# Attention mixer on one core: attention weights in whole products, and the middle of the program planned anew

## Chip, core and metric

One Trainium2 chip, one core. The metric is device time in microseconds (us). The kernel before takes 738.98 us (median of 3 runs, 738.47 to 741.72).

## What is computed

Memory attention in 8 batches of 8 heads, and then a token and channel mixer over the result, all in float32:

```python
a = softmax(phi, axis=2)                       # (8, 8, 576, 32), over the sequence
k_m = einsum('bhsm,bhsd->bhmd', a, k); v_m = einsum('bhsm,bhsd->bhmd', a, v)
attn = softmax(q @ k_m.T / 8)                  # (8, 8, 576, 32)
x = (attn @ v_m) as (8, 576, 512)
h = relu(x.T @ w_tok1) @ w_tok2; u = x + h.T
out = u + relu(u @ w_ch1) @ w_ch2              # 512 -> 1536 -> 512
```

## The kernel before

Float32 accuracy comes from splitting each operand into a high part (rounded by a copy on ACT) and a low part (source minus high, on DVE or POOL); a product is then three products: high by high, high by low, low by high.

**Quads.** Attention goes by quads of four heads: quad `b_Q` is half `Q` of batch `b`. In the middle of the program stand 12 of them, 2_0 to 7_1 (`ThirdBatchQuad` and `LateQuad`). One quad's steps on PE are: `get_kv` (keys and values, 20 narrow products, L452), `turn_T` (L676), `scores` (8 products of 64 rows by 32 columns, L492), `A` (L566), `R` (L572), and for each half of the sequence `attend` (L752) and two `u` (L761). Between them ACT and DVE do softmax and splits, POOL subtracts maxima from `phi` and makes one low part, and the softmax's result goes out to memory and back (`rows_out` L545, `rows_in` L696) to stand in natural order for `A`.

`attend` multiplies the values by the attention weights. The four heads of a quad lie in two pairs of 64 partitions, so each of its six products contracts over 64 rows only, and those of the two pairs (`db` 0 and 1) go to two halves of the array. `a_high` copies all 128 partitions of `aT` on ACT, `a_low` subtracts on DVE.

**Mixer.** The first and second channel layers of chunks 0 to 2 (L146, L169: products of 128 by 128 by 512) are the filler between the quads' steps. Chunks 3 to 8 follow in three pairs (`Pair`, `Run`) by a Strassen scheme, whose weights come as units of 512 KB from memory (`load_unit`, L416): `AHEAD` = 3 units are issued before a run, and then one at each first use of a unit (`Run.first`).

**Order of the work.** `plan` is a list scheduler that runs when the program is built: each `step` has an engine, a cost in us, what it comes after, the rooms (buffers) that it takes, and a rank; `do(t, ...)` gives a quad's step the rank of `t` us after that quad's start, 15.5 us from quad to quad. Engines then run in that order, each strictly in order. `SLACK` is added to what PE and SP wait for, `margin` to a transfer's landing. SP issues nearly all loads; one buffer holds `kv`, so a quad's `kv` is issued only when the quad before it has done `get_kv`. `phi` and the banks `at` and `ch` (two PSUM banks each) have two buffers.

```python
def attend(s, hf):                                   # L745
    w = slice(hf * HALF, (hf + 1) * HALF)
    for x, (v, a) in enumerate(((s.vh, s.ah), (s.vh, s.al), (s.vl, s.ah))):
        for db in range(2):
            own, m = slice(64 * db, 64 * db + 64), slice(db * P, (db + 1) * P)
            nc.tensor.matmul(s.up[db, hf][:, :HALF], v[own, m], a[own, w], start=x == 0, stop=False)
```

Of the kernel before, what the change touches and what calls it, by code (L numbers as in the profile page):

```python
# [10 lines left out]
F32 = mybir.dt.float32  # L11
# [17 lines left out]
def kernel(  # L29
# [37 lines left out]
    WIN, AHEAD = 3, 3  # L67
# [541 lines left out]
    class LateQuad(Quad):  # L609
# [26 lines left out]
        def max_out(s):  # L636
            s.top = dram.tile([1, 4 * M], F32, name="top" + s.n, tag="maxima", bufs=2)
            nc.sync.dma_start(
                out=s.top.rearrange("a (i m) -> (a i) m", m=M), in_=s.turned[:: P // 4, M : 2 * M]
            )  # L640

        def max_in(s):
            s.r = sb.tile([P, 4 * M], F32, tag="pr", name="prr" + s.n, bufs=2)
            nc.sync.dma_start(out=s.r, in_=s.top.to_broadcast([P, 4 * M]))
# [68 lines left out]
        def a_high(s):  # L713
            s.ah = sb.tile([P, S], F32R, tag="ah", name="ah" + s.n, bufs=2)
            nc.scalar.copy(out=s.ah, in_=s.aT)

        def a_low(s, eng):
            s.al = sb.tile([P, S], F32R, tag="ah", name="al" + s.n, bufs=2)
            eng.tensor_tensor(out=s.al, in0=s.aT, in1=f32(s.ah), op=ALU.subtract)
# [25 lines left out]
        def attend(s, hf):  # L745
            w = slice(hf * HALF, (hf + 1) * HALF)
            for db in range(2):
                s.up[db, hf] = bank([P, 512], f"u{db}{hf}" + s.n)
            for x, (v, a) in enumerate(((s.vh, s.ah), (s.vh, s.al), (s.vl, s.ah))):
                for db in range(2):  # L750
                    own, m = slice(64 * db, 64 * db + 64), slice(db * P, (db + 1) * P)
                    nc.tensor.matmul(s.up[db, hf][:, :HALF], v[own, m], a[own, w], start=x == 0, stop=False)  # L752

        def u(s, db, hf):
            m, w = slice(db * P, (db + 1) * P), slice(hf * HALF, (hf + 1) * HALF)
            mm = []
            for t in range(NT):
                h, l = s.Rh[:, t, m], s.Rl[:, t, m]
                mm += [(h, w2h[:, t, w]), (h, w2l[:, t, w]), (l, w2h[:, t, w])]
            for x, (a, r) in enumerate(mm):  # L760
                nc.tensor.matmul(s.up[db, hf][:, :HALF], a, r, start=False, stop=x == len(mm) - 1)  # L761
# [216 lines left out]
    def plan(rank, ways, slow=None, slack=0.0, margin=0.85):  # L978
# [37 lines left out]
        while left:  # L1016
# [4 lines left out]
            if not first:  # L1021
                for z in left:
                    print("STUCK", z.eng, z.fn and z.fn.__code__.co_firstlineno, getattr(getattr(z.fn,"__self__",None),"n",""), z.fn and z.fn.__defaults__, [(r.tags, [(q.tag, sum(u.end is None for u in q.users)) for q in taken.get(r.tags[0][0], [])][-4:]) for r in z.take])
# [594 lines left out]
    class ThirdBatchQuad(SecondQuad):  # L1618

        for name in (  # L1620
            "turn_T", "get_kb", "scores", "S_take", "turn_S", "rows_in", "nat_low", "a_high", "a_low",
            "A", "R", "attend", "u", "straight", "u_high", "u_low", "spill", "store_u",
        ):
            locals()[name] = vars(LateQuad)[name]
# [163 lines left out]
    for z in order:  # L1788
        if z.eng == "PE":
            if z is products[0]:  # L1790
                break
            begin = max(idle, 2.0)
            if z.begin - begin > 0.3 and z.take:

                cold = max(min(z.begin, 5.1) - idle - 1.6, 0.0)
                pace = 0.222 if z.begin < 12.0 else 0.24
                z.fill = int(cold / 0.43 + 0.9 * (z.begin - max(begin, 5.1)) / pace)
            idle = z.end
    for z in order:
        now[0] = z  # L1800
        if z.fn:
            z.fn()

# [3 lines left out]
    def room(tag, n=1):  # L1807
# [8 lines left out]
    kv2, q2, pt2 = room("kv"), room("qT"), room("aT")  # L1816
    begin = step(
        "END", 0, None,
        take=[*sum(c1_rooms, []), *u_rooms[1], o_rooms[0], rest_room, *hidden[0, NF - 1], kv2, q2, pt2],
# [30 lines left out]
    SLACK = 0.4  # L1850
# [8 lines left out]
    def A_LOW(qd):  # L1859
        return "DVE", 0.82, lambda: qd.a_low(nc.vector)  # L1860

    late = [second] + [LateQuad(2, 1)] + [LateQuad(b, Q) for b in range(3, B) for Q in range(2)]
    second_u, former, ends = [], [], {}
    u_done = []
    PERIOD, START, behind, scored, vlows = 15.5, 3.0, [], [begin], []
    for n, qd in enumerate(late):
        t0 = START + PERIOD * n

        def do(t, *args, **kw):
            return todo_at(t0 + t, *args, **kw)  # L1870

        bk, kb, vh, vl, vb, T = room("ch", 2), room("kb"), room("vh", 2), room("vl", 2), Room(("side vb", 1), ("vb", 1)), room("kb") if n else room("pr", 2)
        per = room("ps", 3)
        if n:
            phi_room, kv_r, q_r = room("phi", 2), room("kv"), room("qT")
            r, turned = room("pr", 2), room("al", 2)
            y = do(-32, "SP", 0.45, qd.load_turned, scored[max(n - 2, 0)], take=[turned], move=0.8)
            y.tail = 8.0 if n > 1 else 4.0
            y = do(-27, "DVE", 0.85, qd.phi_max, y, use=[turned])
            y = do(-26, "SP", 0.45, qd.max_out, y, use=[turned], move=0.01)  # L1880
            y.lands, y.tail = True, 2.4
            z = do(-26, "SP", 0.45, qd.load_phi, begin, take=[phi_room], move=0.9)
            y = do(-22, "SP", 0.45, qd.max_in, y, z, take=[r], move=0.1)
            z = do(-16, *PHI_SUB(qd), y, z, use=[phi_room, r], port=True)
            e = do(-13, "ACT", 0.8, qd.phi_only_exp, z, use=[phi_room])
            l = do(-20, "SP", 0.45, qd.load_kv, begin, take=[kv_r], move=3.5)
            lq = do(-12, "SP", 0.45, qd.load_q, begin, take=[q_r], move=1.6)
            kvuse, after = [phi_room, kv_r], [e, l]
        else:
            kvuse, after, q_r, lq = [pt2, kv2], [begin], q2, begin  # L1890
        z = do(-9, "PE", 0.7, qd.get_kv, *after, *former, take=[bk], use=kvuse)
# [12 lines left out]
        aT, ah, al = room("aT"), room("ah", 2), room("ah", 2)  # L1904
        z = do(0, "PE", 1.05, qd.scores, y, lq, take=[*ss, S_], use=[q_r, kb])
        z.not_before = t0
        former, vlows = [z, *vlows[-1:]], vlows + [vlow]
        scored.append(z)
        ends["kv"] = [z]
# [16 lines left out]
        y = do(13, "ACT", 0.7, qd.a_high, t, take=[ah, al], use=[aT])  # L1926
        turned = [y, do(14, *A_LOW(qd), y, use=[aT, ah, al], port=True)]
# [6 lines left out]
        z = do(18, "PE", 0.8, qd.R, z, vlow, *behind, take=[rp], use=[Ah, Al, vh, vl])  # L1934
        z = do(19, "ACT", 0.61, qd.R_high, z, take=[Rh], use=[rp])
        z = do(20, "DVE", 0.7, qd.R_low, z, take=[Rl], use=[rp, Rh])
        last, wrote, stage = z, [[], []], [room(f"stage{db}") for db in range(2)]
        for hf in range(2):
            bks = [room("at", 2) for db in range(2)]
            last = do(20.5 + 2 * hf, "PE", 0.45, lambda qd=qd, hf=hf: qd.attend(hf), z, last, *turned, take=bks, use=[vh, vl, ah, al])  # L1940
            behind = [last]
            n_, to = qd.straight(hf)
            wants = n_ < HALF
            for db, bk in enumerate(bks):
                last = do(
                    21 + 2 * hf + db, "PE", 0.8, lambda qd=qd, db=db, hf=hf: qd.u(db, hf), last, use=[bk, Rh, Rl]
                )
# [145 lines left out]
    order = plan(key, dict.fromkeys(steps, 0), None, SLACK, 2.5)  # L2093
# [43 lines left out]
    class Run:  # L2137
# [151 lines left out]
        def layer_2(s):  # L2289
# [177 lines left out]
```

## Time and profile before

| | |
|---|---|
| median of 3 runs | 738.98 us |
| the profiled execution | 739.23 us, of which 737.4 us are span |
| granted TensorE clock | 0.999 of full speed |
| PE busy | 718.0 us, 4371 products |
| DVE, ACT, POOL busy | 512.5, 349.8, 93.6 us |
| transfers | 155.25 MB, mean 211 GB/s |

Busy time of PE overlaps from product to product, so what a product costs is read from the distance between starts, and what is lost from the waits. A row of the timeline has the start, the duration, the engine, line, operation, output and inputs, rows by columns of the array, the shape, how many, and in brackets the idle time before it and what ended it. The first 120 us hold the loads and quads 0_0 to 1_1; the 12 quads of the middle run from 123 to 380, the three Strassen runs from 383 to the end.

### The profile page before, as it was taken

To read this page: it belongs to the slowest core of one execution; us is meant where nothing else is said; L and a number is where in the kernel's file an instruction comes from. 1 tells how busy PE (TensorE), PEld (TensorE's weight loads), DVE (VectorE), ACT (ScalarE), POOL (GpSimd) and SP (SyncE) were. 2 spreads that over 40 slices of the span, in tenths; PEclk is the share of its full clock that TensorE was granted. 3 is DMA by queue.
4 is the path that set the end of the run, shared out by engine and by line. 5 is a ranking of instruction groups with operands and counts; after the bars stand their busy time and mean duration, and the time that the engine had idled before them with its cause. 6 is when DMAs were issued, how large, how long until landed. Compare 5 with 4: busy or idle time off the path is not lost.

```text
span 737.4 us, 11507 instructions
## 1 busy us (share of the span) xinstructions
PE 718.0 (97%) x4371; PEld 585.7 (79%) x4371; DVE 512.5 (70%) x841; ACT 349.8 (47%) x627; POOL 93.6 (13%) x82
## 2 busy tenths in 40 slices
PE   8999999999999999899997999999999999999998
PEld 8787788777787777688886788887788888788887
DVE  4999854878878797356885648976237977425983
ACT  5999665234344443243443445434345442436450
POOL 2213344222213521100400000000000000000000
PEclk9999999999999999999999999999999999999999
DMA  9965632787979999962436877065559154668302
GB/s 355 415 243 177 219 109 75 235 301 224 289 221 281 322 324 299 321 170 49 163 126 242 304 214 287 29 257 164 185 178 340 48 202 141 199 195 276 129 29 85
DMA packets 99198, 155.25 MB, mean 211 GB/s; under 512 B 38984, under 2 KB 65608, under 8 KB 94792
## 3 DMA queue, kind: packets, MB, share of 16 engines
q1 hardware_dynamic: 88632, 121.37, 48.5%
q10 hardware_dynamic: 10512, 33.17, 14.3%
q8 instruction: 34, 0.56, 0.3%
q14 instruction: 20, 0.16, 0.1%
HBM read 117.34 MB, written 37.16 MB: 210 GB/s over the span
## 4 chain that ended last, share of the span: by engine, by line
PE 63%; DMA 9%; DVE 8%; issue 1%; ACT 1%; POOL 1%; SPq 0%; DVEq 0%; POOLq 0%
PE ma L292 10%; PE mU L2251 10%; PE mB L2251 7%; PE acc L169 6%; PE cp L146 6%; DMA unit<-sums 5%; PE mc L292 5%; PE u L761 4%; PE mD L2251 3%; PE mA L2251 3%; PE Ap L566 2%; PE mb L292 2%; PE u L752 1%; DMA phi<-in_phi_dram 1%; PE kvp L452 1%
## 5 line engine op out<-in xcount | busy, mean ns | idle before, releaser
L169 PE MATMUL acc<-hh,c 128*128 128x512 f32 x288 | 100.0, 396 | 0.0
L169 PEld LDWEIGHTS acc<-hh,c 128*128 128x128 f32 x288 | 54.1, 188 | 12.7 <-issue 2.0
L169 PE MATMUL acc<-hl,c 128*128 128x512 f32 x144 | 56.3, 391 | 0.0
L146 PE MATMUL cp<-uh,c1h 128*128 128x512 f32 x144 | 52.9, 408 | 0.0
L146 PE MATMUL cp<-ul,c1h 128*128 128x512 f32 x144 | 50.5, 391 | 0.0
L146 PE MATMUL cp<-uh,c1l 128*128 128x512 f32 x144 | 50.4, 391 | 0.0
L2237 ACT CAST rT<-hid 128x512 fp32r<-128x512 f32 x54 | 32.0, 621 | 26.8 <-PE mB L2251 15.6
L2238 DVE TENSOR_TENSOR rT<-hid,rT 128x512 fp32r<-128x512 f32 x54 | 35.9, 690 | 7.0 <-ACT rT L2237 7.0
L2105 DVE TENSOR_TENSOR hid<-mb,hid 128x512 f32<-128x512 f32 x12 | 8.3, 692 | 44.6 <-ACT hid L2185 44.6
L711 POOL TENSOR_TENSOR nat<-side,nat 128x512 fp32r<-128x512 f32 (+1 forms) x24 | 24.6, 1026 | 105.7 <-ACT nat L703 99.4
L115 ACT ACTIVATE hh<-cp 128x512 fp32r<-128x512 f32 x36 | 21.5, 596 | 34.3 <-PE cp L146 34.2
L118 DVE SCALAR_TENSOR_TENSOR hl<-cp,hh 128x512 fp32r<-128x512 f32 x36 | 24.6, 684 | 14.0 <-ACT hh L115 14.0
L146 PEld LDWEIGHTS cp<-uh,c1h 128*128 128x128 f32 x144 | 26.5, 189 | 9.4 <-issue 4.9
L2108 ACT ACTIVATE hid<-hid 128x512 f32<-128x512 f32 x24 | 15.2, 633 | 36.2 <-DVE hid L2105 36.2
L146 PEld LDWEIGHTS cp<-uh,c1l 128*128 128x128 f32 x144 | 27.0, 188 | 6.0
L761 PE MATMUL u<-w2h,Rh 128*128 128x288 f32 x96 | 30.8, 321 | 0.0
L146 PEld LDWEIGHTS cp<-ul,c1h 128*128 128x128 f32 x144 | 27.1, 188 | 4.6
L169 PEld LDWEIGHTS acc<-hl,c 128*128 128x128 f32 x144 | 27.1, 188 | 4.4
L292 PE MATMUL ma<-xrest_p,unit 128*128 128x512 f32 x108 | 28.0, 394 | 1.6 <-DMA unit<-sums 1.3
L2237 ACT CAST r<-hid 128x512 fp32r<-128x512 f32 x36 | 22.4, 623 | 14.2 <-PE mU L2251 5.4
L292 PE MATMUL mc<-xw2h_p,unit 128*128 128x512 f32 x72 | 24.6, 395 | 4.5 <-DMA unit<-sums 4.5
L647 POOL TENSOR_TENSOR phi<-phi,prr 128x640 f32<-128x640 f32 x11 | 18.7, 1704 | 80.2 <-DMA prr<-top 33.5
(375 smaller groups left out, 1912.9 us busy)
## 6 DMA issues: line engine op xcount, KB each, us to landing
unit<-sums ACTq DMA_DIRECT2D x54, 512.0 KB, 5.3
kv<-in_kv_dram SPq DMA_DIRECT2D x12, 1300.0 KB, 7.1
rawc<-in_w_ch_dram SPq DMA_DIRECT2D x12, 1024.0 KB, 7.1
q<-in_q_dram SPq DMA_DIRECT2D x16, 576.0 KB, 5.2
sums<-sums SPq DMA_DIRECT2D x12, 512.0 KB, 8.7
u_p<-spilled SPq DMA_DIRECT2D x6, 1024.0 KB, 7.1
phi<-in_phi_dram SPq DMA_DIRECT2D x16, 320.0 KB, 7.5
unit<-sums ACTq DMA_DIRECT2D x18, 256.0 KB, 3.5
```

The lines of the kernel that those rows point to most:

```text
L115: nc.scalar.activation(out=h, in_=ps, func=AF.Relu)
L118: nc.vector.scalar_tensor_tensor(out=l, in0=ps, scalar=0.0, in1=f32(h), op0=ALU.max, op1=ALU.subtract)
L146: nc.tensor.matmul(ps, l[:, a, w], r[:, a], start=n == 0, stop=n == len(mm) - 1)
L169: nc.tensor.matmul(ps, l_[f // 2][:, f % 2, a * P : (a + 1) * P], r[:, w], start=f == start and x == 0, stop=f == end - 1 and x == 2,)
L292: nc.tensor.matmul(ps, l, r, start=first and n == 0, stop=n == len(mm) - 1, skip_group_check=not first,)
L647: eng.tensor_tensor(out=s.pt, in0=s.pt, in1=s.r.rearrange("p (i m) -> p i m", i=4) .unsqueeze(2) .to_broadcast([P, 4, NC, M]), op=ALU.subt ...
L711: eng.tensor_tensor(out=o, in0=a, in1=f32(h), op=ALU.subtract)
L761: nc.tensor.matmul(s.up[db, hf][:, :HALF], a, r, start=False, stop=x == len(mm) - 1)
L2108: nc.scalar.activation(out=to, in_=x, func=AF.Relu)
L2237: nc.scalar.copy(out=t[:, 0], in_=x)
L2238: nc.vector.tensor_tensor(out=t[:, 1], in0=x, in1=f32(t[:, 0]), op=ALU.subtract)
L2251: nc.tensor.matmul(s.banks[room][a][:, w], l_[:, a * P : a * P + P], r_, start=not (p or x) and name in ("11", "T1", "21", "T4"), stop=p = ...
```

## The change

- `attend` goes. `a_high` and `a_low` write, for each pair `p`, one tile of 128 partitions with the pair's high parts in its own 64 partitions and the low parts in the other 64; `v_pair` (four copies of 64 by 128 on ACT) lays the high values twice, one above the other. One product of 128 rows then gives high by high plus high by low, a second one low values by the same tile; both stand at the head of `u`, which starts its own group. `v_pair` is planned behind `R_high`.
- `get_kv` of the next quad is planned directly behind `scores` of this one.
- The middle's ranks: `phi`, its maxima and `kv` are ranked 4 to 12 us earlier, the transposed `phi` of quad 2_1 and its maximum are issued before the middle. `SLACK` 0.4 to 0.8, `margin` 2.5 to 3.5, and `BEHIND`: the planner lets SP issue nothing while landings are more than 2.5 us behind. No instruction waits for that; it sets the order.
- `AHEAD` 3 to 4: four units are issued before the first run, and four instead of three (at steps 35 to 38) before each of the others.

```diff
-    WIN, AHEAD = 3, 3
+    WIN, AHEAD = 3, 4
...
+        def a_high(s, p):
+            if not p:
+                s.pairs = [sb.tile([P, S], F32R, tag="ah", name=f"a{x}" + s.n, bufs=2) for x in range(2)]
+            own = slice(64 * p, 64 * p + 64)
+            nc.scalar.copy(out=s.pairs[p][own], in_=s.aT[own])
+
+        def a_low(s, p, eng):
+            own, other = slice(64 * p, 64 * p + 64), slice(64 - 64 * p, P - 64 * p)
+            t = s.pairs[p]
+            eng.tensor_tensor(out=t[other], in0=s.aT[own], in1=f32(t[own]), op=ALU.subtract)
+
+        def v_pair(s, p):
+            if not p:
+                s.vv = sb.tile([P, 2, P], F32R, tag="Al", name="vv" + s.n, bufs=1)
+            own = slice(64 * p, 64 * p + 64)
+            for x in range(2):
+                nc.scalar.copy(out=s.vv[64 * x : 64 * x + 64, p], in_=f32(s.vh[own, p * P : p * P + P]))
...
         def u(s, db, hf):
+            s.up[db, hf] = bank([P, 512], f"u{db}{hf}" + s.n)
             m, w = slice(db * P, (db + 1) * P), slice(hf * HALF, (hf + 1) * HALF)
-            mm = []
+            a = s.pairs[db][:, w]
+            mm = [(s.vv[:, db], a), (s.vl[:, m], a)]
...
+            if z.eng == "SP":
+                t = max(t, landed.get("SP", 0.0) - behind)
...
+        z = do(0, "PE", 1.0, qd.scores, y, qd.lq, take=[*ss, S_], use=[qd.q_r, kb])
+        if nx:
+            got_kv = do(0.1, "PE", 1.25, nx.get_kv, z, *nx.after, *vlows[-1:], take=[bank_rooms[n + 1]], use=nx.kvuse)
...
-                    (35, load_unit), (36, load_unit), (37, load_unit),
+                    (35, load_unit), (36, load_unit), (37, load_unit), (38, load_unit),
```

On PE, where quad 4_1 multiplies its values by the attention weights; before (names are tile, batch, quad, number):

```order
L752 MATMUL u00_4_1_3002<-ah_4_1_2870,vh_4_1_2614 128x288
L752 MATMUL u10_4_1_3003<-ah_4_1_2870,vh_4_1_2614 128x288
L752 MATMUL u00_4_1_3002<-al_4_1_2900,vh_4_1_2614 128x288
L752 MATMUL u10_4_1_3003<-al_4_1_2900,vh_4_1_2614 128x288
L752 MATMUL u00_4_1_3002<-ah_4_1_2870,vl_4_1_2625 128x288
L752 MATMUL u10_4_1_3003<-ah_4_1_2870,vl_4_1_2625 128x288
L761 MATMUL u00_4_1_3002<-w2h_96,Rh_4_1_2957 128x288
```

and of the change:

```order
L764 MATMUL u00_4_1_3103<-a0_4_1_2851,vv_4_1_3076 128x288
L764 MATMUL u00_4_1_3103<-a0_4_1_2851,vl_4_1_2678 128x288
L764 MATMUL u00_4_1_3103<-w2h_96,Rh_4_1_3068 128x288
L764 MATMUL u00_4_1_3103<-w2l_97,Rh_4_1_3068 128x288
L764 MATMUL u00_4_1_3103<-w2h_96,Rl_4_1_3079 128x288
```

Six products of half the rows ahead of two `u` have become two whole ones at the head of each `u`; the four `u` of a quad now mostly stand back to back. From the last product of `R` to the first of `u` there are 6 to 15 mixer products before (most often 9; in four quads `get_kv` besides), and now 15, or 9 to 12 and `get_kv` or an `A` besides.

On PE, the scores of quad 6_0 (`sp`) and the keys and values of 6_1 (`kvp`); before:

```order
L492 MATMUL sp1_6_0_3145<-q_6_0_2951,kb_6_0_3092 32x288
L146 MATMUL cp2_2_3128<-uh_2_1385,c1h2_611 128x512
L146 MATMUL cp2_2_3128<-ul_2_1386,c1h2_611 128x512
L146 MATMUL cp2_2_3128<-uh_2_1385,c1l2_612 128x512
L146 MATMUL cp2_2_3128<-uh_2_1385,c1h2_611 128x512
```

and of the change:

```order
L492 MATMUL sp0_6_0_3199<-q_6_0_2933,kb_6_0_2981 32x288
L492 MATMUL sp1_6_0_3200<-q_6_0_2933,kb_6_0_2981 32x288
L452 MATMUL kvp_6_1_3214<-kv_6_1_2945,phi_6_1_2854 32x130 x20
L572 MATMUL Rp_5_0_3242<-vh_5_0_2781,Ah_5_0_3179 128x256
L572 MATMUL Rp_5_0_3242<-vl_5_0_2849,Ah_5_0_3179 128x256
```

Before, `kvp` of 6_1 stood 13 rows behind these scores, after mixer products and an `R`. Of 11 such places 7 are joined now; before, 3 were, and one `get_kv` stood directly before an `attend`.

On ACT, the unit loads where the first Strassen run begins; before:

```order
L416 DMA unit011_4299<-sums1_1380 128x1024
L2185 COPY hidal_0_4295<-ma00_4315 128x512
L2108 ACTIVATE hidal_0_4295<-hidal_0_4295 128x512
L416 DMA unit002_4335<-sums0_1379 128x1024
L2191 COPY hidal_0_4296<-mc00_4334 128x512
L2194 COPY hidaT_0_4297<-ma00_4315 128x512
L416 DMA unit012_4353<-sums1_1380 128x1024
```

and of the change:

```order
L416 DMA unit002_4337<-sums0_1385 128x1024
L2216 COPY hidal_0_4333<-ma00_4353 128x512
L2139 ACTIVATE hidal_0_4333<-hidal_0_4333 128x512
L416 DMA unit012_4373<-sums1_1386 128x1024
L2222 COPY hidal_0_4334<-mc00_4372 128x512
L2225 COPY hidaT_0_4335<-ma00_4353 128x512
L416 DMA unit020_4391<-sums2_1387 128x1024
```

Each unit's load stands where the one before it stood.

## Rows read from the trace of the kernel before

**Rows 1.** The page: busy time of each engine, share of the span, instructions.

```profile
PE 718.0 (97%) x4371; PEld 585.7 (79%) x4371; DVE 512.5 (70%) x841; ACT 349.8 (47%) x627; POOL 93.6 (13%) x82
```

**Rows 2.** Waits of PE, 60 to 400: who for whom, us, times, longest.

```profile
PE mc L292 <- DMA unit<-sums: 3.9, 2, 2.1
PE kvp L452 <- ACT phi L446: 3.3, 2, 1.8
PE u L752 <- DVE Rl L118: 2.2, 1, 2.2
...
PE kvp L676 <- DVE side L1145: 0.2, 1, 0.2
```

**Rows 3.** Waits of PE, 400 to the end.

```profile
PE ma L292 <- DMA unit<-sums: 1.3, 3, 0.6
PE mc L292 <- DMA unit<-sums: 0.6, 2, 0.4
```

**Rows 4.** Timeline of PE: the keys of 7_1, and a product that waits for a unit.

```profile
314.10 1.32 PE L452 MATMUL kvp<-kv,phi 128*32 128x130 f32 x40 [1.49 <-ACT phi L446]
...
396.54 0.39 PE L292 MATMUL mc<-xw2h_p,unit 128*128 128x512 f32 x1
398.75 0.47 PE L292 MATMUL mc<-xw2h_p,unit 128*128 128x512 f32 x1 [1.82 <-DMA unit<-sums]
```

**Rows 5.** Stretches: length, busy PE, PEld, DVE, ACT, POOL; clock, DMA share, GB/s.

```profile
125.00:225.00 100.00, 99.36 (x768) 77.99 (x768) 77.49 (x145) 36.36 (x79) 19.58 (x15) 1.00 0.83 259
225.00:303.00 78.00, 73.82 (x632) 58.03 (x630) 60.07 (x109) 32.48 (x70) 20.46 (x16) 1.00 0.97 308
```

**Rows 6.** Timeline of PE around one `attend`.

```profile
190.23 0.39 PE L146 MATMUL cp<-ul,c1h 128*128 128x512 f32 x1
190.46 0.39 PE L146 MATMUL cp<-uh,c1l 128*128 128x512 f32 x1
190.78 0.40 PE L752 MATMUL u<-ah,vh 64*128 64x288 f32 x2
...
191.61 0.29 PE L761 MATMUL u<-w2l,Rh 128*128 128x288 f32 x1
191.74 0.29 PE L761 MATMUL u<-w2h,Rl 128*128 128x288 f32 x1
```

**Rows 7.** Timeline of PE: scores alone, keys alone, both joined (last four rows).

```profile
198.78 0.39 PE L169 MATMUL acc<-hh,c 128*128 128x512 f32 x1
...
200.08 0.39 PE L146 MATMUL cp<-ul,c1h 128*128 128x512 f32 x1
...
207.53 0.39 PE L169 MATMUL acc<-hh,c 128*128 128x512 f32 x1
...
209.43 0.39 PE L146 MATMUL cp<-ul,c1h 128*128 128x512 f32 x1
...
172.05 0.39 PE L146 MATMUL cp<-uh,c1l 128*128 128x512 f32 x1
172.37 0.72 PE L492 MATMUL sp<-q,kb 64*32 64x288 f32 x16
173.02 1.32 PE L452 MATMUL kvp<-kv,phi 128*32 128x130 f32 x40
...
174.60 0.39 PE L146 MATMUL cp<-ul,c1h 128*128 128x512 f32 x1
```

**Rows 8.** Groups on ACT, 30 to 130: quads 1_0 and 1_1, already in pairs.

```profile
L1524 ACT CAST a<-aT 64x576 fp32r<-64x576 f32 x4 | 2.7, 674 | 0.2
...
L538 ACT CAST vv<-vh 64x128 fp32r<-64x128 f32 x8 | 2.4, 298 | 0.1
```

**Rows 9.** High and low attention weights, L715 and L719: ns least, median, most.

```profile
L715 ACT CAST ah<-aT x12: 668/671/677, 139.6 to 351.5; 128x576 fp32r<-128x576 f32 x12
...
L719 DVE TENSOR_TENSOR al<-aT,ah x12: 743/758/1662, 140.3 to 352.8; 128x576 fp32r<-128x576 f32 x12
```

**Rows 10.** Timeline of ACT's queue: loads of units as the first run begins.

```profile
383.81 0.33 ACTq L416 DMA_DIRECT2D unit<-sums  x1
...
387.95 0.84 ACTq L416 DMA_DIRECT2D unit<-sums  x2
```

More of the change, by code (lines that the diff above doesn't have):

```diff
@@ L1798 @@
             idle = z.end
+    late = [second] + [LateQuad(2, 1)] + [LateQuad(b, Q) for b in range(3, B) for Q in range(2)]
+    ahead = [(quads[1, 0].x_u[3].end, late[1].load_turned)] + [(118.0, fn) for fn in (late[1].phi_max, late[1].max_out)]
     for z in order:
+        while ahead and z.begin > ahead[0][0]:
+            ahead.pop(0)[1]()
         now[0] = z
@@ L1802 @@
             z.fn()
+    assert not ahead
     steps.clear()
@@ L1816 @@
     kv2, q2, pt2 = room("kv"), room("qT"), room("aT")
+    turned1 = room("al", 2)
     begin = step(
         "END", 0, None,
[L1819 removed]
+        take=[*sum(c1_rooms, []), *u_rooms[1], o_rooms[0], rest_room, *hidden[0, NF - 1], kv2, q2, pt2, turned1],
     )
@@ L1857, in NAT_LOW @@
         return "POOL", 1.8, lambda: qd.nat_low(nc.gpsimd)
[L1859 to L1865, printed above, removed]
-    for n, qd in enumerate(late):
[L1867 to L1880, printed above, removed]
-            y.lands, y.tail = True, 2.4
[L1882 to L1891, printed above, removed]
@@ new lines, with later @@
+    second_u, ends, u_done = [], {}, []
+    PERIOD, START = 15.5, 3.0
+    first, scored, vlows, ahead = [begin], [begin], [], []
+    bank_rooms = [room("ch", 2) for qd in late]
+    kb_rooms, vh_rooms, vl_rooms = ([room(tag, m) for qd in late] for tag, m in (("kb", 1), ("vh", 2), ("vl", 2)))
+    def later(n):
+        t0 = START + PERIOD * n
+        return t0, lambda t, *args, **kw: todo_at(t0 + t, *args, **kw)
+    for n, qd in enumerate(late):
+        t0, do = later(n)
+        if not n:
+            qd.kvuse, qd.after, qd.q_r, qd.lq = [pt2, kv2], [begin], q2, begin
+            continue
+        phi_room, kv_r, q_r = room("phi", 2), room("kv"), room("qT")
+        if n == 1:
+            y, turned = begin, turned1
+        else:
+            turned = room("al", 2)
+            y = qd.l_turned = do(TURN_AT, "SP", 0.45, qd.load_turned, begin, take=[turned], move=0.8)
+            y.tail = 8.0 if n > 2 else 4.0
+            y = do(-36, "DVE", 0.85, qd.phi_max, y, use=[turned])
+            y = do(-35, "SP", 0.45, qd.max_out, y, use=[turned], move=0.01)
+            y.lands, y.tail = True, 2.4
+        z = do(-30, "SP", 0.45, qd.load_phi, begin, take=[phi_room], move=0.9)
+        r = room("pr", 2)
+        y = do(-28, "SP", 0.45, qd.max_in, y, z, take=[r], move=0.1)
+        z = do(-21, *PHI_SUB(qd), y, z, use=[phi_room, r], port=True)
+        e = do(-20, "ACT", 0.8, qd.phi_only_exp, z, use=[phi_room])
+        l = do(-28, "SP", 0.45, qd.load_kv, begin, take=[kv_r], move=3.5)
+        qd.lq = do(-12, "SP", 0.45, qd.load_q, begin, take=[q_r], move=1.6)
+        qd.kvuse, qd.after, qd.q_r = [phi_room, kv_r], [e, l], q_r
@@ L1892 @@
+    t0, do = later(0)
+    got_kv = do(-9, "PE", 1.25, second.get_kv, begin, take=[bank_rooms[0]], use=second.kvuse)
+    for n, qd in enumerate(late):
+        t0, do = later(n)
+        bk, kb, vh, vl, vb = bank_rooms[n], kb_rooms[n], vh_rooms[n], vl_rooms[n], Room(("side vb", 1), ("vb", 1))
+        T, per = room("kb") if n else room("pr", 2), room("ps", 3)
+        z = got_kv
         if n:
@@ L1925 @@
         ends["S"] = [t, z]
-        y = do(13, "ACT", 0.7, qd.a_high, t, take=[ah, al], use=[aT])
-        turned = [y, do(14, *A_LOW(qd), y, use=[aT, ah, al], port=True)]
+        turned = []
+        for p in range(2):
+            y = do(12 + p, "ACT", 0.69, lambda qd=qd, p=p: qd.a_high(p), t, *turned[:1], use=[aT, *ah] if p else [aT], take=[] if p else ah)
+            turned += [y, do(14 + p, "DVE", 0.8, lambda qd=qd, p=p: qd.a_low(p, nc.vector), y, use=[aT, *ah], port=True)]
         ap, Ah, Al = room("at", 2), room("Ah"), room("Al")
```

77 lines of the change are left out of this document (35 added, 42 removed).

## The prediction

> **What bounds the kernel now.** I read the page's first part, then PE's waits, then PE's timeline at the places that the change touches, then the stretches. PE is busy 718.0 of 737.4 us [rows 1]: it is the bound, and a gain is either less PE work or fewer PE waits. PE's waits have two kinds. From 60 to 400 there are eight entries, 11.3 us in all, of which the first three and the last stand here [rows 2]: 3.9 us are two waits for units of the Strassen run, and 7.4 us belong to the quads, chiefly keys that wait for `exp(phi)` (3.3 us) and a `u` that waits for `R`'s low part (2.2 us). Behind 400, five more waits for units cost 1.9 us [rows 3]. The view undercounts: the wait shown as 1.82 us lies between starts 2.21 us apart, where 0.23 is usual, so it costs 1.98, or 0.16 more [rows 4, 6]. With 0.16 for each, the seven waits for units cost 5.8 + 1.1 = **6.9 us**, and the eight of the quads 7.4 + 1.3 = **8.7 us**. The longest of the latter lie where the transfer engines are full: their share is 0.83 from 125 to 225 and 0.97 from 225 to 303 [rows 5].
>
> **What the change does, part by part.**
>
> *Attention weights, PE.* An `attend` group: the last mixer product ahead starts at 190.46, the second `u` product behind at 191.61, 1.15 us [rows 6]. Without the group it would be 0.23 (one mixer product, 190.23 to 190.46) and 0.13 (one `u` product, 191.61 to 191.74): the group costs 0.79 us. There are 24 (12 quads, two halves): 19.0 us. In their place come 12 x 4 x 2 = 96 whole products at the `u` pace, 0.133 us: 12.8 us. Gain **6.2 us**.
>
> The row is odd: six half products cost 0.79 us, as much as six whole ones, though each two start together (one entry "x2") and the second and third pair follow quickly; the surplus stands at the entry and exit, where the array goes from 128*128 to 64*128 and back. The Trainium skill (TensorEngine Tiling (Array Packing), Theoretical Speedup) says that a contraction of 64 or less runs up to twice as fast when two tiles work side by side: that speaks against this change. By it alone the group would cost three passes, 0.40 us, and the change would lose 12.8 - 9.6 = 3.2 us. The trace has the pairs side by side and the 0.79 all the same; the same page (Key Properties) says that a change of tiling mode drains the array, and by that sentence the trace agrees.
>
> *Scores and keys joined, PE.* Less two mixer products (0.46), scores alone cost 200.08 - 198.78 - 0.46 = 0.84, keys alone 209.43 - 207.53 - 0.46 = 1.44, and both joined 174.60 - 172.05 - 0.46 = 2.09 [rows 7]: a join saves 0.19. By the order 7 are joined instead of 3 joins and one `get_kv` against an `attend`: three more, **0.6 us**. The words of the change promise eleven; the order gives seven.
>
> *ACT and DVE.* Per quad ACT gets 2 x 0.674 for 0.671 us and 4 x 0.298 us more, +1.87 us; DVE 2 x 0.76 for 0.76 us [rows 8, 9]. That DVE takes as long for 64 partitions as for 128 I take from ACT's rows, which do. Over 125 to 303 ACT is busy 68.8 us and DVE 137.6 of 178 [rows 5]; some ten quads add 19 and 8 us: 49% and 82%. Both have room; PE work covers it, so I cost it at nothing. What could become late: `u` now begins with `vv`, which ACT makes behind `R_high` (1.19 us against 0.70 for DVE's low part). The order puts 15 mixer products (3.4 us) or their like between `R` and `u`, where 9 (2.1 us) were usual and one quad waited 2.2 us [rows 2]. So this wait goes rather than grows. If DVE's `a_low` meets POOL it can take 1.66 us [rows 9], 0.9 more twice per quad, off PE's path unless the softmax behind it is late.
>
> *Units.* The loads move one slot ahead. In the first run the slots are at 383.81 and 387.95 [rows 10]: the unit whose product waited at 395 was issued at 387.95 and now at 383.81, and so on in each run. A wait is at most 2.1 us [rows 2], this slot 4.1. The fourth load before the first run takes a buffer that a store must leave first, and ACT stands until then; between `A` and `R` of quad 6_1, where it stands, the order has twelve mixer products and scores, 3.6 us, before ACT's next result is due. Bounds: nothing of the 6.9 us left, or, where ACT's queue or the full transfers eat the lead, 4 us left. I take 0.9 left: **6.0 us** gained.
>
> *The middle's order.* No row shows what waits are left under the new order; I bound it. At best none: 8.7 us gained. The other bound comes from the transfers. From 125 to 303 they work 0.83 x 100 + 0.97 x 78 = 158.7 us [rows 5], 0.89 of the time, on all that the keys of 7_1 need; those keys began at 314.1, 189 us behind 125 [rows 4]. In the new order PE has less to do up to there (9 mixer products, 16 `attend` groups against 64 whole products, three joins: 2.0 + 4.1 + 0.6 = 6.7 us), and without the waits of the quads only 189 - 6.7 - 8.3 = 174 us are left (all but the last 0.5 us of the waits, that of an `R`, lie ahead of that place). In these go the 158.7 us of transfers and some 2 us of sums that the order moved ahead: a share of 0.92. At the 0.97 of the full stretch 160.7 us take 166, and nothing waits; at the 0.89 of before they take 181, and 6 to 7 us of waits are left. The new ranks start every chain of `phi` earlier, which speaks for the first end; a wait in a new place, which this count doesn't see, for the second. I take about the middle between both ends, 3.7 left: **5.0 us** gained.
>
> *Sum.* 6.2 + 0.6 + 6.0 + 5.0 = 17.8 us, against the profiled execution's 739.23 (0.25 above the median of the runs): **721.4 us**.
>
> **The rivals.**
>
> *The transfers stay the bound.* The waits of the quads stay as they are, in new places, since the transfer engines give no more than the 0.97 of 225 to 303 [rows 5] and a new order at 0.92 leaves no room for a bad turn: 739.2 - 6.2 - 0.6 - 6.0 = 726.4; with half as much again, 731. For it: the keys then come as late as before. Against it: the 0.83 before 225, where room is.
>
> *The fourth unit doesn't help*: loads are issued earlier but land behind the stores of the sums' tops and of chunk 2, or wait for a buffer. 721.4 + 6 = 727.4. For it: the two long waits of the first run, while the transfers are busy with other things [rows 2]. Against it: the later runs' waits are all 0.6 or less [rows 3], so a slot is ample there.
>
> *Half products are cheap*: what a group costs is not the mode but something that stays, and the term is +3.2 instead of -6.2: 730.8. Against it: the surplus stands exactly at the change of shape [rows 6], and joins save one such change [rows 7]. The Trainium skill's rule on half contractions (the same page and section) would lead here.
>
> *Slower: two banks for four `u`.* The four `u` of a quad stand back to back on two banks, so the third can't start before ACT has copied the first out, and the fourth not before the second. That leaves about 1.07 us (eight products) for a copy. ACT is strictly in order, with a `nat` copy that waits for a transfer, or casts of full width, between such copies. It decides from (17.8 + 3.7)/12 = 1.8 us per quad; at 2.3 us the time is 749. Against it: ACT is half idle [rows 5], and the order has the copies mostly together.
>
> **How the numbers follow.** The forecast (waits of quads and units within 2 or 3 us of what I took, 717 to 724.5) gets 0.62; transfers 0.22; units 0.08; half products 0.02; two banks 0.04; 0.02 for a time below 717. The best case is 739.2 - 6.8 - 6.9 - 8.7 = 716.8. The range 716 to 729.5 takes in that end and the two larger rivals without the former's tail. A measurement of this kernel tells some 0.5%, 3.7 us, from no change. Below 735.3 lie all but the slower rival and a piece of the transfers' tail together with bad luck on the units: faster 0.93, same 0.03, slower 0.04.
>
> **What would show it.** In the changed profile: no products of 64 by 128 behind 123 us, and eight products per `u` at 0.13 us without a jump at entry; PE's 4371 products 48 fewer; joins at 2.1 us; waits for units under 1 us in all; waits of the quads 2 to 5 us, with a transfer share over 0.9 already from 145 on. Wrong would be: PE waiting at the third `u` of a quad for ACT; waits for `kv` or `phi` above 8 us; ACT standing at a unit load while `R`'s high part is due.

## The result, and the profile after

The changed kernel takes 729.08 us (median of 4 runs, 727.64 to 731.11), the kernel before 740.28 on the same chip: a ratio of 0.985, with a 95% interval of 0.981 to 0.989. That is faster by 1.5%, clear of the noise, and inside the range of 716 to 729.5 by 0.4 us. The forecast of 721.4 itself is missed: between the profiled executions 11.0 us are gained (739.23 to 728.23) and not the 17.8 of the sum.

The page of the changed kernel, which answers to [rows 1]: 48 products fewer, as forecast, and more for DVE and ACT to do.

```profile
PE 711.4 (98%) x4323; PEld 591.9 (81%) x4323; DVE 524.2 (72%) x853; ACT 369.7 (51%) x687; POOL 91.8 (13%) x82
```

**Where the time went, by stages.** I cut each execution at two products: the first keys of quad 2_0, where the middle begins, and the first product into `ma`, as the Strassen runs begin. From PE's timeline, of the kernel before:

```profile
123.47 1.30 PE L1491 MATMUL kvp<-kv,pt 128*32 128x128 f32 x40
...
382.15 0.39 PE L292 MATMUL ma<-xqT_p,unit 128*128 128x512 f32 x1
```

and of the changed kernel:

```profile
124.06 1.30 PE L1493 MATMUL kvp<-kv,pt 128*32 128x128 f32 x40
...
379.97 0.39 PE L292 MATMUL ma<-xqT_p,unit 128*128 128x512 f32 x1
```

The middle went from 258.7 us to 255.9, the rest, up to the end of the span, from 355.3 (737.4 - 382.15) to 346.5 (726.5 - 379.97). So 8.8 us of the 11.0 come from the rest, and the middle, in which the forecast had 11.8 (6.2 + 0.6 + 5.0), gave 2.8; 0.6 were lost ahead of it. The rest is settled quickly: behind 400 PE's waits have no entry left, where [rows 3] stood. The middle needs the waits, which answer to [rows 2] (PE, 60 to 400: who for whom, total, times, longest):

```profile
PE Rp L572 <- DVE Al L741: 1.9, 1, 1.9
PE sp L492 <- ACT side L774: 1.8, 1, 1.8
PE u L764 <- DVE ul L195: 1.7, 2, 1.4
PE sp L492 <- DVE Al L741: 1.3, 2, 1.1
PE kvp L676 <- DVE side L1147: 0.9, 1, 0.9
PE u L764 <- ACT side L774: 0.7, 2, 0.5
PE Rp L572 <- DVE S L690: 0.7, 1, 0.7
PE Rp L572 <- ACT Ah L737: 0.3, 1, 0.3
```

These are 9.3 us, all of the quads, against 7.4 before. None is for a unit, none for `exp(phi)`: every one names a result of DVE or a copy of ACT. The stretches, which answer to [rows 5] (length, busy PE, PEld, DVE, ACT, POOL, granted clock, share of the transfers, GB/s):

```profile
125.00:225.00 100.00, 96.73 (x799) 78.33 (x788) 82.11 (x153) 45.23 (x104) 19.66 (x17) 1.00 0.87 272
225.00:303.00 78.00, 73.91 (x587) 60.52 (x586) 60.22 (x106) 37.23 (x85) 20.03 (x16) 0.98 0.94 301
```

The transfers moved forward about as forecast: their share ahead of 225 went from 0.83 to 0.87, and from 145 to 225 it is 0.89, where over 0.9 was expected. The largest loss of the middle lies in one place, scores and keys joined at 292. PE's timeline there:

```profile
290.39 0.40 PE L146 MATMUL cp<-uh,c1l 128*128 128x512 f32 x1
292.59 0.67 PE L492 MATMUL sp<-q,kb 64*32 64x288 f32 x2 [1.80 <-ACT side L774]
294.31 1.21 PE L492 MATMUL sp<-q,kb 64*32 64x288 f32 x14 [1.05 <-DVE Al L741]
295.45 2.24 PE L452 MATMUL kvp<-kv,phi 128*32 128x130 f32 x40
297.62 0.38 PE L572 MATMUL Rp<-vh,Ah 128*128 128x256 f32 x1
```

From the last mixer product to `R` are 7.23 us. A join that doesn't wait takes 2.21 from the last mixer product to the next step (186.47 - 184.26, in the rows on joins further down), so 5.0 us are lost. The scores need both `at` banks. One holds a `u` of 5_0, which ACT has to copy out (`side`, L774), the other the `A` of 5_1, which DVE has to read (`Al`). ACT's timeline says why that is late:

```profile
287.61 0.40 ACT L774 COPY side<-u 128x288 f32<-128x288 f32 x1 [2.11 <-PE u L764]
291.51 0.74 ACT L446 ACTIVATE phi<-phi 128x640 f32<-128x640 f32 x1 [3.50 <-POOL phi L647]
292.16 0.38 ACT L774 COPY side<-u 128x288 f32<-128x288 f32 x1
```

ACT stood 3.5 us for `exp(phi)`, with the copy queued behind it. POOL, which makes that `phi`, stood for a transfer:

```profile
289.93 1.55 POOL L647 TENSOR_TENSOR phi<-phi,r 128x640 f32<-128x640 f32 x1 [11.79 <-DMA r<-top]
```

This `phi` is the one of 7_1, whose keys PE takes up only at 310, so nobody needed it yet. DVE's timeline shows the same for the other bank: `Al` stands behind the first mix of the first pair (L251), whose operand was still on its way.

```profile
292.36 1.23 DVE L251 TENSOR_TENSOR t<-u_p,u_p 128x1024 f32<-128x1024 f32 x1 [5.78 <-DMA u_p<-spilled]
293.50 0.42 DVE L481 TENSOR_TENSOR vl<-side,vh 128x256 fp32r<-128x256 f32 x1
293.84 0.42 DVE L741 TENSOR_TENSOR Al<-Ap,Ah 128x256 fp32r<-128x256 f32 x1
```

The longest single wait, 1.93 us of an `R` for `Al` that ends at 362.86, is of another kind: no transfer stands there. DVE had two sums for the first pair ahead of `Al`, and took 2.92 us over them beside POOL (timelines of DVE and POOL):

```profile
359.55 2.92 DVE L308 TENSOR_TENSOR cw<-c 128x256 f32<-128x256 f32 x2
362.40 0.41 DVE L741 TENSOR_TENSOR Al<-Ap,Ah 128x256 fp32r<-128x256 f32 x1
```

```profile
356.09 6.10 POOL L180 TENSOR_TENSOR o<-uh,ul 128x512 f32<-128x512 f32 x4
```

So the theory with which I went on: **queues in order**. The plan puts a step that waits for a transfer, and that nothing needs soon, ahead of the short copies that free a bank, and PE pays. Its rivals: **transfers** (the waits only show that the loads can't come faster, and would come back elsewhere), **added work** (the copies and low parts that whole products want, which I had costed at nothing) and, later, a **draw** (any order that the planner makes has some such places, and how many is chance).

### The profile page after: what moved, and what is told of

It reads as the page before. It is cut to its first block, busy times and chain, and to the rows that moved or that the text cites. A ratio compares the mean times of both kernels' runs of the same rounds, so it can differ in the third digit from the quotient of the medians.

```text
span 726.5 us, 11468 instructions
## 1 busy us (share of the span) xinstructions
PE 711.4 (98%) x4323; PEld 591.9 (81%) x4323; DVE 524.2 (72%) x853; ACT 369.7 (51%) x687; POOL 91.8 (13%) x82
## 4 chain that ended last, share of the span: by engine, by line
PE 84%; DMA 6%; DVE 5%; SPq 2%; POOL 1%; issue 1%; ACT 1%; DVEq 0%; POOLq 0%; ACTq 0%
PE ma L292 13%; PE cp L146 11%; PE acc L169 11%; PE mU L2282 10%; PE mB L2282 7%; PE mc L292 7%; PE u L764 4%; PE mD L2282 3%; PE mA L2282 3%; PE mb L292 3%; DMA kv<-in_kv_dram 3%; PE Ap L566 2%; PE kvp L452 2%; DMA u_p<-spilled 1%; PE Rp L572 1%; PE sp L492 1%
## 5 line engine op out<-in xcount | busy, mean ns | idle before, releaser
L2268 ACT CAST r<-hid 128x512 fp32r<-128x512 f32 x36 | 22.4, 623 | 14.2 <-PE mU L2282 5.4
L774 ACT COPY side<-u 128x288 f32<-128x288 f32 (+1 forms) x44 | 17.0, 391 | 24.1 <-PE u L764 20.7
L2269 DVE TENSOR_TENSOR r<-hid,r 128x512 fp32r<-128x512 f32 x36 | 24.7, 685 | 5.1 <-ACT r L2268 4.8
L764 PE MATMUL u<-w2h,Rh 128*128 128x288 f32 x96 | 28.3, 295 | 0.0
L764 PE MATMUL u<-w2l,Rh 128*128 128x288 f32 x96 | 28.3, 295 | 0.0
```

Source lines behind the costliest of these rows:

```text
L764: nc.tensor.matmul(s.up[db, hf][:, :HALF], a, r, start=x == 0, stop=x == len(mm) - 1)
L774: nc.scalar.copy(out=side[0][:, o + n : o + HALF], in_=ps[:, n:HALF])
L2268: nc.scalar.copy(out=t[:, 0], in_=x)
L2269: nc.vector.tensor_tensor(out=t[:, 1], in0=x, in1=f32(t[:, 0]), op=ALU.subtract)
```

## The experiments

All runs in one table: median time, its ratio to the kernel before on the same chip, length of the middle and of the rest, the sum of PE's waits shown in the middle, and the granted clock over the profiled execution. The last four come from that one execution; in e5 it is the slowest of four (731.12), in e12 the fastest of four (718.70).

| run | us | ratio (95%) | middle | rest | waits | clock |
|---|---|---|---|---|---|---|
| before | 740.28 | | 258.7 | 355.3 | 7.4 | 0.999 |
| changed | 729.08 | 0.985 (0.981 to 0.989) | 255.9 | 346.5 | 9.3 | 0.998 |
| e1 units only | 732.62 | 0.988 (0.984 to 0.993) | 259.4 | 346.5 | 6.9 | 0.997 |
| e2 whole products only | 747.32 | 1.008 (1.004 to 1.011) | 269.4 | 351.8 | 14.9 | 0.984 |
| e3 changed, half products | 727.35 | 0.981 (0.976 to 0.986) | 253.9 | 346.8 | 3.5 | 0.998 |
| e4 two steps moved | 725.60 | 0.979 (0.975 to 0.983) | 253.0 | 346.5 | 7.3 | 0.998 |
| e5 changed, again | 730.10 | 0.987 (0.982 to 0.991) | 257.7 | 346.5 | 8.8 | 0.993 |
| e6 eleven steps moved | 722.23 | 0.976 (0.972 to 0.980) | 248.8 | 346.5 | 5.1 | 1.000 |
| e7 half products, same work | 729.71 | 0.986 (0.983 to 0.990) | 259.2 | 346.5 | 7.4 | 0.998 |
| e8 `A` behind `u` | 727.91 | 0.984 (0.979 to 0.989) | 254.9 | 346.5 | 9.5 | 0.998 |
| e9 price of `u` | 738.69 | 0.997 (0.993 to 1.000) | 265.3 | 346.5 | 15.9 | 0.993 |
| e10 price of the mixer | 748.84 | 1.014 (1.010 to 1.018) | 276.6 | 346.5 | 22.4 | 0.986 |
| e11 half products, mixer's price | 737.16 | 0.997 (0.994 to 0.999) | 264.8 | 346.5 | 11.2 | 0.990 |
| e12 more steps moved | 721.88 | 0.976 (0.972 to 0.981) | 246.5 | 346.5 | 3.7 | 0.999 |

**e1: the fourth unit by itself**, on the kernel before.

```diff
-    WIN, AHEAD = 3, 3
+    WIN, AHEAD = 3, 4
...
-                    (35, load_unit), (36, load_unit), (37, load_unit),
+                    (35, load_unit), (36, load_unit), (37, load_unit), (38, load_unit),
```

> The kernel before, with the fourth unit load alone. If the seven waits for units are all that the fourth load removes: 6.9 us off, 733.4 against some 740.3 for the kernel before, no wait for a unit left behind 380, quads' waits as before (7.4 us shown). If the loads only land behind other transfers: 3 us or less off, with waits for units of 2 us left in the first run.

The rest takes 346.5 us, as in every kernel with four units (346.5 to 346.8), and 355.3 before: 8.8 us, more than the 6.9 that I had counted, with no wait for a unit left. The middle stays (259.4). So the fourth unit by itself gives what the rest of the changed kernel gained. What three units lose isn't fixed, though: in e2, which has three, the rest takes 351.8.

**e2, e3, e7: whole or half products.** e2 is the kernel before with the whole products' functions and steps. e3 is the changed kernel with `attend` and the undivided `a_high` and `a_low` of before. e7 is e3 with ACT's and DVE's work of the changed kernel; the copies of values are extra and change nothing in the result:

```diff
+        def v_pair(s, p):
+            own = slice(64 * p, 64 * p + 64)
+            for x in range(2):
+                v = s.vh[own, p * P : p * P + P]
+                nc.scalar.copy(out=v, in_=f32(v))
```

> The kernel before, with whole products alone (old ranks, old slack and margin, three loads). If the products are the whole effect: 6.2 us off, 734. If the added copies and low parts on ACT and DVE make quads wait (rival: added work): the waits of the quads rise from 7.4 shown to 10 or more and 3 us or less are left of the gain, 737 or above. Unit waits stay at 5.8 shown. The plan is made anew, so two or three us of other waits may come or go in either case.

> The changed kernel with the half products put back (attend, one high and one low part), all else as changed. If the added work on ACT and DVE makes the middle's waits: they fall from 9.3 shown to under 5, and the time is 730 or less, since the products' 6.2 come back and 4 or more of waits go. If the new order makes them: waits of about 9, with the 6.2 on top, 734.5.

> The changed kernel with half products, but with ACT and DVE doing the same work as for whole ones: a's high and low parts in two steps of 64 partitions each, v's part copied four times (onto itself), at the same places. If the added work makes the waits: the waits of the run with half products (3.5 us shown) rise to 8 or more and the time from 727 to 731 or more. If what makes them is where the whole products put things (vv in Al's room, four u one behind the other on two banks): waits stay under 5 and the time at 726 to 728.5.

Whole products alone made the kernel slower, and without them the changed kernel is as fast as with them: the middle takes 253.9 us, with 3.5 us of waits. By my line of e3's expectation that spoke for added work. e7 (7.4 us of waits, 729.71) fell between its two lines, nearer to added work, but 3.9 of its waits are a single wait of keys for `exp(phi)`, whose POOL step stood for the transfer `r<-top`: not the added work. Every one of these kernels had been planned anew, so I had to know what planning anew does by itself.

**e9, e10, e11: another order for the same work.** One price in the planner moved by 0.01 us, in the changed kernel (e9, e10) and in e3 (e11). No instruction is added or taken away.

```diff
-                    20.5 + 2 * db + hf, "PE", 1.07, lambda qd=qd, db=db, hf=hf: qd.u(db, hf), z, last, *turned,
+                    20.5 + 2 * db + hf, "PE", 1.06, lambda qd=qd, db=db, hf=hf: qd.u(db, hf), z, last, *turned,
```

e10 and e11 have 0.68 for 0.69 in `first_layer` and `second_layer` instead.

> The changed kernel with one price of the planner moved by a hundredth: a u costs 1.06 instead of 1.07 (the trace has 8 x 0.133 = 1.064). No work changes, yet the planner gives another order. If a new order's waits are a draw: the quads' waits shown lie anywhere from 3 to 13 us (9.3 in the changed kernel) and the time from 722 to 732. If the waits are set by transfers or by added work: 9 to 10 shown and 728 to 730.

> The changed kernel with another price moved by a hundredth: three mixer products cost 0.68 instead of 0.69 (the trace has 3 x 0.227 = 0.681). As for the price of u: a draw gives waits from 3 to 13 us and 722 to 732, transfers or added work 9 to 10 and 728 to 730.

> The kernel of the run with half products (waits 3.5 us shown, 727.4), with the same price moved, 0.68 instead of 0.69. If its few waits were a lucky draw: they rise to 5 or more and the time to 729 or more. If half products leave few waits whatever the order, since ACT and DVE have less to do: under 5 shown and 726 to 728.5.

It is a draw, and a wider one than I expected: with the same work the time goes from 729 to 738.7 and to 748.8, slower than the kernel before, and the waits from 9.3 to 22.4; the low waits of e3 weren't owed to the half products either (11.2 in e11).

In e10 the waits aren't all of it. Its granted clock is 0.986 over 746.2 us and the changed kernel's 0.998 over 726.5; if what is missing from 1 cost PE in proportion, that is at most 10.4 us against 1.5 (an estimate). With 13.1 us more of waits it covers the 20.7 by which the middle is longer. All three moved prices came out slower than the price that they replaced, so the orders that I started from may be better than most; three are too few to tell.

The share of the transfers from 225 to 303 lies at 0.93 to 0.97 in these three, in e3 and in the changed kernel, and tells nothing of it. So e2, e3 and e7 don't settle what the added work costs, nor does e2's loss show whole products to be slower. The first of PE's waits in e9, and what ACT did there (its timeline):

```profile
PE u L764 <- ACT side L774: 7.1, 3, 6.2
```

```profile
318.43 0.62 ACT L703 CAST nat<-side 128x512 fp32r<-128x512 f32 x1 [7.79 <-DMA side<-rows]
...
319.62 0.69 ACT L774 COPY side<-u 128x288 f32<-128x288 f32 x2
```

and in e11 (timeline of ACT), where PE stood 7.2 us for the same kind of copy:

```profile
307.53 0.30 ACT L704 CAST nat<-side 64x128 fp32r<-64x128 f32 x1 [5.85 <-DMA side<-rows]
...
312.32 0.40 ACT L771 COPY side<-u 128x288 f32<-128x288 f32 x1 [4.00 <-DMA spilled<-side]
```

In e9 it is again a copy that frees a bank, behind a step of ACT that stands for a transfer. In e11 only the first part is that: PE has stood since 305.57, ACT's `nat` stands for its load until 307.53, and then the copy itself stands 4.00 us for the store that empties its own buffer (`side`). In e10 the largest are scores that wait for `q` itself:

```profile
PE sp L492 <- DMA q<-in_q_dram: 5.6, 2, 3.1
PE u L764 <- ACT side L774: 4.8, 2, 2.8
...
```

The `q` of the longer of the two was issued by SP at 303.14 only, 4.8 us ahead of the scores at 307.94.

**e4: two steps moved, PE's order kept.** To hold the order still, I moved steps by hand behind the plan, each behind another on its own engine (`by` keeps them by name).

```diff
+    for z, y in (
+        (by["exp", "_7_1"], by["vv", "_5_1"]), (by["t1"], by["al", "_5_1"]),
+    ):
+        order.remove(z)
+        order.insert(order.index(y) + 1, z)
```

> The changed kernel, two steps moved by hand and PE's order untouched: ACT's exp of phi for quad 7_1 behind the v pairs of 5_1, DVE's first mix of the first pair behind a's low parts of 5_1. If engines that stand in order behind a transfer which nothing needs yet make the wait at 292 (theory: in-order queues): PE's pauses of 1.8 and 1.1 us there go, the block of 7.1 us takes 2.1 to 2.5, and the time falls by 4.5 to 5, to some 723.5 where the changed kernel takes 728.2. If the transfers are the bound: the time comes back as waits of later keys (7_0, 7_1), 727 or more. If added work makes it: nothing changes.

Both pauses are gone, and nothing came back at the keys of 7_0 or 7_1. The time, 725.60, lies between the 723.5 expected and the 727 of the transfers, since of the 5.0 us 1.2 stayed in another wait: `R`, directly behind the joined keys, now stood for the turning of the scores on DVE, behind `a`'s two low parts (1.72 us) and the mix (1.23). PE's timeline:

```profile
290.65 0.72 PE L492 MATMUL sp<-q,kb 64*32 64x288 f32 x16
291.30 1.32 PE L452 MATMUL kvp<-kv,phi 128*32 128x130 f32 x40
293.80 0.39 PE L572 MATMUL Rp<-vh,Ah 128*128 128x256 f32 x1 [1.18 <-DVE S L690]
```

**e8: a rule instead of a move.** `vv` stands in the room of `Al`, so the plan held the `A` of 5_1 in its bank until the last `u` of 5_0.

```diff
-        z = do(15, "PE", 1.75, qd.A, z, take=[ap], use=[nat])
+        z = do(15, "PE", 1.75, qd.A, z, *ends.get("u", ()), take=[ap], use=[nat])
```

> The changed kernel with one more rule for the planner: A of a quad behind the last u of the quad ahead, since A's low part can't be written while vv stands in its room. Only from A of 5_1 on does the order change. If the shared room makes the wait at 292 (A's bank held for 9 us): that wait goes, 5 us less, 723 to 725, apart from what the new order brings. If it is ACT's and DVE's standing behind transfers alone: waits of 3 us or more stay between 280 and 320 and the time at 727 or more.

The bank is free now, and PE waits at the same place, 3.5 us for the turning of the scores: ACT still stands 4.79 us for that `phi`, and DVE, which does the turning, 3.72 for the pair's load. So a wait of this size needs no shared room; the steps standing for transfers are what it has in common with the changed kernel. What the room cost of the 5.0 us isn't shown, as e8 is planned anew.

**e5, e6, e12: the moves carried on.** e6 (its label says nine) moves eleven steps at six places, the order of PE, POOL and SP untouched; e12 takes in three more places.

```diff
+        (by["exp", "_7_1"], by["vv", "_5_1"]), (by["t1"], by["Rl", "_5_1"]),
+        (by["sum", 1], by["ul", "_2_0", 0, 1]), (by["high", 1], by["uh", "_2_0", 1, 0]), (by["low", 1], by["ul", "_2_0", 1, 0]),
+        (by["top", 3, 1], by["Al", "_7_1"]), (by["top", 3, 0], by["Al", "_7_1"]),
+        (by["words", 2], by["turn", "_4_0"]), (by["high", 3], by["uh", "_3_1", 0, 1]),
+        (by["al", "_4_0"][3], by["Al", "_4_0"]), (by["al", "_4_0"][1], by["Al", "_4_0"]),
```

In e12 the last line is replaced by:

```diff
+        (by["St", "_4_1"], by["turn", "_5_0"]), (by["al", "_4_0"][3], by["turn", "_5_0"]), (by["al", "_4_0"][1], by["turn", "_5_0"]),
+        (by["St", "_6_0"], by["turn", "_6_1"]), (by["al", "_5_1"][3], by["turn", "_6_1"]), (by["al", "_5_1"][1], by["turn", "_6_1"]),
+        (done["T1"][1], by["Rl", "_7_1"]), (done["11"][1], by["Rl", "_7_1"]),
```

> The changed kernel as it is, for a comparison on the chip of the other three: every theory expects the 0.985 of before that it had, 728 to 730.

> The changed kernel, eleven steps of ACT and DVE moved by hand at six places where PE waited (exp of phi for 7_1 and the pair's first mix as before, now behind R's low part; the sums of pair 1 behind two u copies; two sums of tops behind A's low part of 7_1; the words of pair 2 behind the turning of S; a cast of sums 3 behind a u copy; a's low parts of 4_0 behind A's low part), PE's, POOL's and SP's order untouched. If engines that stand in order make the waits: 5.0 + 1.6 + 2.1 + 0.7 + 0.7 + 0.7 = 10.8 us less than the changed kernel at best, 8 expected: 719 to 721. If transfers are the bound: the waits come back at later keys or u and over 725 is left. If added work is, 725 or more too, since no work is taken away.

> The run with eleven steps moved (722.2), with more at three places where PE still waited: a's low parts and the turning of the weights of the quad ahead behind the turning of S, for 5_0 and 6_1, and two low parts of the first pair behind R's low part of 7_1. If DVE's order makes these waits: 1.3 + 1.0 + 0.9 us go, 2.5 expected, some 719.5. If DVE lacks time there, the waits move to the u that need a's low parts: 721.5 or more.

Against the changed kernel on the same chip (e5) e6 is 7.9 us faster (722.23, a little over the 719 to 721 expected). Its middle is 8.9 us shorter than e5's and 7.1 shorter than that of the changed kernel's first trace, whose clock was higher. The transfers, their order and the work of every engine are the same. That rules out transfers and added work as a bound that held the time of these places. What it doesn't show is that the moved steps stood for transfers: two of the eleven did, those at 292. The other nine, at five places, are sums, casts and low parts of DVE and ACT that nothing needed soon and that were simply long, such as the two sums ahead of `Al` at 362. (For one of them, a cast, the view puts 0.79 us down to a load, but the sum that it reads ended just then.) Between e4's middle and e6's lie 4.2 us, at most 1.4 of them by the clock. So the theory holds in a wider form: PE pays for any step that isn't needed soon and stands or works ahead of a short one that is.

e12's three waits are gone as well, and its middle is another 2.3 us shorter in its fastest run, but others came up at `u`, 2.0 us for ACT's copies and 0.6 for `R`'s low part. Its four runs spread from 718.7 to 724.2, the median of 721.88 is over the 719.5 expected and no better than e6's beyond doubt. Both beat the changed kernel and the one before.

## Why the prediction was right or wrong

*Attention weights on PE: right.* A `u` now takes 1.06 us for eight products without a jump at entry. PE's timeline of the changed kernel, from the last product of `A` over one `u` to the transpose behind it:

```profile
280.56 0.28 PE L566 MATMUL Ap<-w1l,nat 128*128 128x256 f32 x1
280.68 0.30 PE L764 MATMUL u<-a,vv 128*128 128x288 f32 x1
...
281.74 0.27 PE L676 MATMUL kvp<-ident,T 128*128 128x128 f32 x1
```

So the term of 6.2 us stands, by the same count of rows, and the rival that half products are cheap falls. The table bears it out under every order: the middle, less its waits and less the span times what the clock lacks of 1 (an estimate of the clock's cost), is 242.1 to 245.1 us in the nine runs with whole products and 246.2 to 250.6 in the five with half products, 243.7 and 249.3 in the mean; two of the five also have fewer joins.

*Joins: right.* Seven instead of three, and those that don't wait cost 2.09 as in [rows 7]: here 186.71 - 184.26 - 0.23 (the mixer product) - 0.13 (the first `u` product) = 2.09.

```profile
184.26 0.39 PE L146 MATMUL cp<-uh,c1l 128*128 128x512 f32 x1
184.58 0.72 PE L492 MATMUL sp<-q,kb 64*32 64x288 f32 x16
185.23 1.32 PE L452 MATMUL kvp<-kv,phi 128*32 128x130 f32 x40
186.47 0.40 PE L764 MATMUL u<-a,vv 128*128 128x288 f32 x1
186.71 0.30 PE L764 MATMUL u<-a,vl 128*128 128x288 f32 x1
```

*Units: right in kind, too small.* 8.8 us instead of 6.0 (e1). Nothing was left over, and by the distance of starts the trace of before has nine such waits, 7.6 us, where I had counted seven; the other 1.2 are in ones too short for the view.

*The middle's order: wrong, and this is the step that failed.* "At best none: 8.7 us gained. The other bound comes from the transfers." I took 3.7 us as left. Left were 12.9: 9.3 shown, 2.15 more in the block at 292 (5.0 lost, 2.85 shown), and 0.16 for each of nine other waits. The sum then comes out nearly: 6.2 + 0.6 off and 4.2 on (8.7 to 12.9) make 2.6 for the middle, where 2.8 was measured. Three things were wrong in it. The bound was no bound: a share of the transfers tells whether the loads can come in time on the whole, not whether some engine stands for one of them; with the share at 0.93 to 0.97 the waits went from 3.5 to 22.4 us. The count allowed for waits in new places ("which this count doesn't see") without a price for them, and those were what came. And the line that "the new ranks start every chain of `phi` earlier, which speaks for the first end" had the wrong sign where it mattered: `exp(phi)` of 7_1 stood so early in ACT's queue that a copy for 5_0 waited behind it. Of the signs named for the forecast the share of the transfers came close (0.89 from 145 to 225, 0.91 from 145 to 303), and the waits of the quads failed: 9.3 us instead of 2 to 5.

*ACT and DVE, "I cost it at nothing": not settled.* The doubled low parts are ahead of what PE waited for in e4, but orders with and without the added work overlap (3.5, 7.4 and 11.2 us of waits with half products; 9.3, 9.5, 15.9 and 22.4 with whole ones).

*The rivals, and luck.* Three rivals gave times as near as 1.7 to 2.7 us to the measured 729.08, and none had the cause: "The transfers stay the bound" (726.4), which e6 and e12 refute; "The fourth unit doesn't help" (727.4), which e1 refutes; "Half products are cheap" (730.8). "Two banks for four `u`" came nearest to the mechanism, a copy behind a longer step of ACT, and got 0.04 and 749 us: in the changed kernel such a copy held the scores at 292 and a `u` only for 0.7 us in all, in e9 one `u` waits 6.2 us for it, and in e10 two wait 4.8 us, the second behind a cast that stood for DVE and for no transfer. That a tuned price in the planner decides between these I didn't see. The range held by luck: it reached to the larger rivals, the 2.8 us that the units gave beyond the forecast made up for part of the 9.0 that the middle lacked, and the same kernel measured again (e5) takes 730.10, outside the range.

## What to carry to other kernels

Where a program is ordered by a planner, an edit that lets it plan anew is two edits: the work, which rows can price, and a new order, whose waits are a draw. Here that draw was worth up to 20 us for a price moved by 0.01, so compare edits at a fixed order, or over several orders. In an order that is kept, look at each wait for what its releaser's engine stood for or worked on: a step that is needed late, because it waits for a transfer or is just long, belongs behind the short steps that PE needs next. Moving eleven such steps by hand gave 8 us without touching PE or the loads.

## What was not expected of the hardware

**A wait can cost more than it shows, through the clock.** In the block at 292 the 40 products of `kvp` took 2.24 us, where 1.32 is usual. The stretches there show the granted clock (third column from the end) at 0.50, the lower of its two levels, right behind the two pauses:

```profile
292.00:294.00 2.00, 0.67 (x2) 0.13 (x2) 1.64 (x3) 1.77 (x4) 0.00 (x0) 1.00 1.03 284
294.00:296.00 2.00, 1.69 (x26) 0.74 (x30) 1.94 (x4) 0.00 (x0) 0.00 (x0) 0.50 1.00 326
296.00:298.00 2.00, 2.00 (x39) 1.65 (x32) 1.94 (x4) 0.00 (x0) 0.00 (x0) 0.65 1.01 318
```

It need not happen: the wait of 1.93 us of the last `R` for `Al` was followed by a clock of 1.00 in the changed kernel, and in the same kernel run again (e5, where it ends at 364.16) by this:

```profile
364.00:366.00 2.00, 1.84 (x7) 1.64 (x8) 2.00 (x5) 0.83 (x3) 0.00 (x0) 0.62 0.00 0
366.00:368.00 2.00, 2.00 (x6) 1.51 (x6) 2.00 (x3) 1.06 (x4) 0.00 (x0) 0.52 0.00 0
```

**DVE beside POOL.** Four sums of 128 by 256 take 1.55 us on DVE by themselves and took 4.03 while POOL worked from 169.72 to 173.33 (timelines of DVE and POOL of the changed kernel). One by one, the first three end at 171.31, 171.91 and 173.61, each 0.28 us behind the end of a POOL instruction; the `u` at 174.36, the third of its quad, waited 1.4 us for the low part behind them.

```profile
169.91 4.03 DVE L368 TENSOR_TENSOR sums<-sums 128x256 f32<-128x256 f32 x4
...
282.08 1.55 DVE L368 TENSOR_TENSOR sums<-sums 128x256 f32<-128x256 f32 x4
```

```profile
169.72 1.90 POOL L711 TENSOR_TENSOR nat<-side,nat 128x512 fp32r<-128x512 f32 x2 [11.08 <-ACT nat L703]
171.70 1.62 POOL L647 TENSOR_TENSOR phi<-phi,r 128x640 f32<-128x640 f32 x1
```

The Trainium skill (SBUF — State Buffer, "SBUF: two separate sides") says that DVE and GpSimd (POOL) share a pair of ports that one instruction holds for its whole length while the other waits, for a DVE instruction with two inputs in SBUF against a GpSimd one that reads SBUF. The rows agree: three sums ended just behind a POOL instruction, and the fourth, when POOL was done, took 0.41 us. The planner counts such steps as exclusive, but it places them by its own times, and here POOL's began when their data came. The two sums ahead of `Al` at 362, too, took 2.92 us beside POOL.
